# Second MLP: output product by seven block products, decoding inside PSUM, fixed ring slots

## The chip, the cores and the metric

One core of one Trainium2 chip. A core has five engines with instruction streams of their own: TensorE (PE: matmuls, with weight loads listed as PEld), VectorE (DVE), ScalarE (ACT), GpSimd (POOL) and SyncE (SP), which here issues the DMA transfers. Matmuls write to PSUM, a memory of eight banks; a bank holds 512 float32 columns on 128 partitions. VectorE and ScalarE read PSUM, GpSimd doesn't. The metric is the device time of one launch in microseconds, lower is better. This kernel was run three times: 957.83, 962.25 and 962.66 us.

## The reference

Three stages in float32, the output of one being the input of the next.

```python
# attention, 4 batches, 8 heads, 576 positions, 64 wide; causal by blocks of 64
attn = softmax(where(block_i >= block_j, q @ k.T / 8, -1e9));  x = attn @ v      # x: 2304 tokens x 512
# first MLP, 512 -> 2048 -> 512
h = x @ w_in;  x = (h * tanh(softplus(h))) @ w_out
# second MLP, 512 -> 1536 -> 512, with RMS norm
xn = x / sqrt(mean(x * x) + 1e-6) * rms_g
out = (silu(xn @ w_gate) * (xn @ w_val)) @ w_out
```

Inputs and weights come as 64-bit floats and are turned into 32-bit ones on the chip.

## The kernel before

**Precision.** A float32 operand is kept as two float16 halves, high and low. A product is three passes: high with high, high with low, low with high (`PASSES`).

**Second MLP, gate and value.** It runs by row blocks `n` (18 of them). Two row blocks, 256 rows of the hidden layer, are a block `l` = `n // 2` (9 of them); `l` goes over 3 weight blocks `fq` of 512 hidden rows and, inside each, 3 token blocks `p` of 768 tokens. In a row block, gate and then value are computed by a scheme of seven block products for eight (Strassen's, in Winograd's form): `quads("g")`, then `quads("v")`. The left operands are the weights (seven combinations, tiles of `row`, called `pair_row` outside), the right ones the normed tokens (seven combinations, 14 float16 column groups, loaded by transposing DMAs in `load_xn`). A `product` is 6 matmuls of 384 columns (L1790) into a PSUM bank of its own; the banks come in turn from two rings of two, `h` and `s`. The four results are put together outside PSUM: `copied` (ScalarE, L1808), `plus` (VectorE, L1818: a product read from PSUM plus a tile) and `both` (a sum of two tiles, VectorE or GpSimd, L1828). Gate results pass through Silu (L1840), value results are multiplied by them (L1846), and the product is split into a high half (L1853, L1854) and a low half (L1856): the tiles `pp`, in four rings of three or two.

**Second MLP, output.** `mlp2_o(l, pps)` multiplies the `pp` tiles of two row blocks by a block of `w_out`, as plain products: six output tiles of 128 tokens x 512 columns, for each 4 x 3 matmuls of 512 columns (L1925) into one of three banks. With `fq` = 0 ScalarE copies the bank into an accumulator in SBUF (L1935); after that VectorE adds to it (L1942). After the last `fq` the tile is stored (L1950).

**Weights.** `stage_w2` loads the three weights of one `fq`, rebuilds float32 from the 64-bit words by three integer operations on VectorE (L578, L586, L606), finds scales, and splits them; for `w_out` it makes two halves of the four plain pieces (`split`, L544 and L551). The next `fq` is staged while the present one is computed; for the last there is nothing to stage.

**Order of the work.** Nothing is issued in the order of the text. All operations are recorded first (`Plan.op`) with their engine or a choice of engines, an estimated duration and a due time (`at`). `Plan.place` simulates the engines with these estimates and takes, on each engine, the ready operation of the smallest key; `Plan.run` repeats that forward and backward for some rounds, adds tabled shifts (`SHIFT` by part of the program, `FINE` by operation), keeps the shortest plan and issues each engine's instructions in its order. At run time an engine follows that fixed order and waits at semaphores. An operation that reuses a tile of a ring waits for all uses of the tile that had the place before; in the second MLP the planner also holds the first use of a tile behind the first use of the tile before it in the ring (`b.after`). The products of gate and value, and the `plus` operations, are chained in their order (`chain`).

Of the kernel before, what the change touches and what calls it, by code (L numbers as in the profile page):

```python
# [47 lines left out]

class Buf:


    def __init__(self, pool, shape, dtype, name, tag, bufs):
        self.pool, self.shape, self.dtype, self.name, self.tag, self.bufs = pool, shape, dtype, name, tag, bufs
        self.ap, self.acc, self.prev, self.cols, self.whole, self.after = None, [], None, None, None, None
# [36 lines left out]
class Plan:  # L91


    def __init__(self):
        self.ops, self.rings, self.part, self.ordered = [], {}, "", False
# [16 lines left out]
    def op(self, eng, ns, fn, r=(), w=(), at=0.0, alts=(), after=(), table=None, issue=T_DGE):  # L112
# [15 lines left out]
        for acc, wr in ((r, False), (w, True)):  # L128
            for a in acc:
                b, part = split_part(a)  # L130
                if b.after is not None and not b.acc:
                    o.deps.update(p for p, _, _ in b.after.acc[:1])
                b.acc.append((o, part, wr))
# [4 lines left out]
    def place(self, key, back=False):  # L138
# [23 lines left out]
        while left:  # L162
# [160 lines left out]
def t_rows(n, nbytes):  # L323

    return n * {256: 12.0, 2048: 6.44, 4096: 13.44}[nbytes]
# [3 lines left out]
def block_attention_mish_mlp_gated_mlp(  # L329
# [37 lines left out]
    STEP2 = 21500.0  # L367
# [117 lines left out]
    def pow2_of_norm(cols, s, e, at, sl=ALL):  # L485
# [9 lines left out]
        pow2(c, None, (s, sl), (e, sl), 13, at)  # L495
# [295 lines left out]
    def split_k(b, a, pace):  # L791
# [6 lines left out]
        for tt in range(NTT):  # L798
# [9 lines left out]
                DMA, 1540.0 * n / P,  # L808
# [57 lines left out]
    def prep_q(b, tt, at):  # L866
# [15 lines left out]
        else:  # L882
# [13 lines left out]
            DMA, 1540.0 * n / P,  # L896
# [4 lines left out]
        op(DMA, 400, lambda: nc.sync.dma_start(out=w()[0:D, :, :n], in_=a()[D:P, :, :n]), r=[a], w=[(w, 0)], at=at)  # L901
        op(DMA, 400, lambda: nc.sync.dma_start(out=w()[D:P, :, :n], in_=a()[0:D, :, :n]), r=[a], w=[(w, 1)], at=at)
# [40 lines left out]
    def attention(b, i, at, pace):  # L943
# [113 lines left out]
        def probs(keys, es, at):  # L1057
# [50 lines left out]
            for z, e in enumerate(es):  # L1108
# [24 lines left out]
                DMA, 1.5 * wd,  # L1133
# [35 lines left out]
        def norm_x(half, xt, at):  # L1169
# [56 lines left out]
            if last:  # L1226
                for hh in range(2):
                    for s_ in range(2):
                        op(
                            DMA, 400,  # L1230
# [15 lines left out]
            for t, c0, jl, w in runs:  # L1246
                if t not in x16:
                    x16[t] = buf("m1", [P, 2 * NCC, T1], F16, f"x16_{t}", "x16", X_BUFS)
                op(
                    DMA, 770.0 * w,  # L1250
# [26 lines left out]
    op(DMA, 800, lambda: nc.sync.dma_start(out=rgb(), in_=rms_g.partition_broadcast(P)), w=[rgb], at=60000)  # L1277
# [183 lines left out]
    def norm(t, m, at):  # L1461
# [37 lines left out]
        def halves(pool, o0, o1, c0, part):  # L1499
# [4 lines left out]
            else:  # L1504
# [16 lines left out]
                DMA, {2: 824, 3: 1250}[w],  # L1521
# [58 lines left out]
    plan.ordered = True  # L1580
# [24 lines left out]
    def stage_w2(fq, at, pace, o_at, o_pace):  # L1605
# [4 lines left out]
        def stage(nm, src, z, at=at, pace=pace):  # L1610
# [18 lines left out]
            if nm == "o":  # L1629
                pow2_of_norm(sq, w2s[nm], w2E[nm], a, sl)  # L1630
# [16 lines left out]
            if nm == "o":  # L1647
                d = w2[nm, fq] = buf("m2", [P, FQ, 2, FW], F16, f"w2{nm}{fq}", f"wo{fq % 2}", 1)
                for cc in range(FQ):
                    split(  # L1650
                        lambda d=d, cc=cc: d()[:, cc, 0, :], lambda d=d, cc=cc: d()[:, cc, 1, :],
                        lambda big=big, cc=cc: big()[:, cc, :], s_, FW, d, [(big, cc), (w2s[nm], fq)], a, (cc, 1), (cc, 0),
                    )
# [10 lines left out]
        def row(nm, r, a):  # L1664
            plan.part = f"r{nm}{fq}_{r}"
            big = bigs[nm]
            y = (NR * fq + r) % 3
            d = w2[nm, fq, r] = buf("m2" if y == 2 else "w2", [P, 7, 2, 2, P], F16, f"w2{nm}{fq}_{r}", f"w{nm}{y}", 1)
# [3 lines left out]
            def put(o, r, src, rd):  # L1672
                hi, lo_ = lambda: d()[:, o, 0], lambda: d()[:, o, 1]
                n = 2 * P
                op(
                    ACT, t_act(n), lambda: nc.scalar.activation(out=hi(), in_=src(), func=AF.Copy), r=rd, w=[(d, (o, 0))],  # L1676
# [4 lines left out]
                    POOL, t_pool(n), lambda: lo(nc.gpsimd), r=rd + [(d, (o, 0))], w=[(d, (o, 1))], at=a,  # L1681
# [3 lines left out]
            def summed(o, r, i0, i1, rd, fn):  # L1685
                x = buf("w2", [P, 2, P], F32, f"w2s{nm}{fq}_{r}_{o}", "wsum6" if o == 3 else f"wsum{o}", 1)
# [10 lines left out]
            put(0, r, q[1, 1], rk_[1])  # L1697
            put(1, r, q[1, 2], rk_[2])
            put(2, r, q[2, 2], rk_[2])
            s1_ = summed(4, r, q[2, 1], q[2, 2], rk_[1] + rk_[2], ALU.add)  # L1700
            s2_ = summed(5, r, s1_, q[1, 1], [s1_] + rk_[1], ALU.subtract)
            summed(6, r, q[1, 1], q[2, 1], rk_[1], ALU.subtract)
            summed(3, r, q[1, 2], s2_, [s2_] + rk_[2], ALU.subtract)

        def scales_gv(a):
# [17 lines left out]
                    out=ck()[:, sl], in0=w2E["v"]()[:, sl], scalar1=gr(), scalar2=2.0**-16, op0=ALU.mult, op1=ALU.mult  # L1723
# [4 lines left out]
        def scale_o(a):  # L1728
# [7 lines left out]
            tiny(lambda: nc.vector.tensor_scalar_mul(co()[:, sl], g2(), 2.0**-15), [g2], [(co, fq)], a)  # L1736

        bigs = {}
        return (
            lambda: (stage("g", w_gate, 0), stage("v", w_val, FQ), scales_gv(at + pace * 2 * FQ)),  # L1740
            lambda r, a: (row("g", r, a), row("v", r, a)),
            lambda: (stage("o", w_out2, 0, o_at, o_pace), scale_o(o_at + o_pace * FQ)),
        )
# [3 lines left out]
    def load_xn(l, at):  # L1747
# [4 lines left out]
        for part, c0, c1 in ((0, 0, 2 * DM), (1, 2 * DM, 4 * DM), (2, 4 * DM, 7 * DM)):  # L1752
            for m in range(NM):
                r0 = (p * NM + m) * P
                op(
                    DMA, 1.5 * (c1 - c0),
# [8 lines left out]
    chain = {"PE": [], "DVE": [], "n": 0}  # L1765
    PRODUCTS = {1: (0, 0), 2: (1, 1), 3: (3, 2), 4: (2, 6), 5: (4, 3), 6: (5, 4), 7: (6, 5)}

    def mlp2_gv(n):
# [6 lines left out]
        def quads(nm):  # L1775
# [3 lines left out]
            bank = {}  # L1779

            def product(z):
                wo, xo = PRODUCTS[z]
                chain["n"] += 1
                b = bank[z] = (ps_h if chain["n"] % 2 else ps_s)([P, T2], f"{nm}{n}_{z}")

                def mm():
                    i = 0
                    for cc in range(2):
                        for wh, xh in PASSES:
                            nc.tensor.matmul(  # L1790
                                b(), w()[:, wo, wh, cc, :], x()[:, (2 * xo + xh) * 2 + cc, :],
                                start=(i == 0), stop=(i == 5),
# [4 lines left out]
                chain["PE"] = [op(PE, t_mm(T2, 6), mm, r=xs + [(w, (wo, 0)), (w, (wo, 1))], w=[b], at=a, after=chain["PE"])]  # L1797

            scale = (lambda: 1.0) if nm == "g" else (lambda: ck()[:, fq : fq + 1])
            sc_r = [] if nm == "g" else [(ck, fq)]  # L1800

            def copied(z, tag):

                d = buf("w2", [P, T2], F32, f"{tag}{nm}{n}", tag, 1)
                b = bank[z]
# [6 lines left out]
            def plus(z, u, name, d=None):  # L1812

                d = d or buf("w2", [P, T2], F32, f"{name}{nm}{n}", name, 1)
                b = bank[z]
                last = op(
# [4 lines left out]
                    r=[b] + ([] if d is u else [u]) + sc_r, w=[d], at=a, after=chain["DVE"],  # L1821
                )
                chain["DVE"] = [last]
                return d

            def both(u, v, name, d=None):
                d = d or buf("w2", [P, T2], F32, f"{name}{nm}{n}", name, 1)
                f = lambda eng: eng.tensor_tensor(out=d(), in0=u(), in1=v(), op=ALU.add)  # L1828
                op(
                    POOL, t_pool(T2), lambda: f(nc.gpsimd), r=[u] if d is v else [u, v], w=[d], at=a,  # L1830
                    alts=[(DVE, t_dvett(T2), lambda: f(nc.vector))],
                )
                return d

            def use(i, src):

                if nm == "g":
                    op(
                        ACT, t_act(T2, 1),
                        lambda: nc.scalar.activation(out=src(), in_=src(), func=AF.Silu, scale=cg()[:, fq : fq + 1]),  # L1840
# [358 lines left out]
```

## Time and profile before

| | |
|---|---|
| runs | 957.83, 962.25, 962.66 us; median 962.25 |
| the profiled execution | 958.27 us |
| its span, first to last instruction | 956.5 us |
| mean granted TensorE clock | 0.999 of full |
| instructions | 18899 |

The profile shows one execution. Busy time is the time in which an engine had at least one instruction in flight; matmuls are pipelined, so the mean duration of one is longer than the distance from one to the next. The first 550 us hold attention and the first MLP, interleaved; the second MLP begins at 557 us, and its last matmul ends 3.9 us before the span does.

### The profile page before, as it was taken

The numbers are of one execution on the slowest core, as the hardware profiler recorded it, in microseconds if no ns is written. First come the engines' busy times: TensorE is split into PE (matmuls) and PEld (weight loads), VectorE is DVE, ScalarE is ACT, GpSimd is POOL, SyncE is SP. The second block draws the span as 40 slices with busy tenths as digits, with TensorE's granted clock in tenths as the row PEclk, the third lists the DMA queues.
The fourth block names the chain that finished last, engine by engine and source line by source line (L and its number), as shares of the span: only waits on it lengthen the run. The fifth ranks groups of instructions, "written<-read, shape, count | busy, mean of one in ns | idle before, by whom it ended". The sixth has DMA issues, their size and how long they took to land. (4 is left out here: it accounts for less than half of the span.)

```text
span 956.5 us, 18899 instructions
## 1 busy us (share of the span) xinstructions
PE 932.2 (97%) x6754; PEld 585.3 (61%) x6755; DVE 785.3 (82%) x1797; ACT 600.5 (63%) x1244; POOL 509.9 (53%) x659
## 2 busy tenths in 40 slices
PE   8999999899999999999999999999999999999998
PEld 7785566466666758666675665555555555545553
DVE  5999978987896689988884999899989989765654
ACT  4769679998699889887775654647454635312320
POOL 1249245885562447577551936768555856412321
PEclk9999999999999999999999999999999999999999
DMA  9754698699875498788663747755658270552002
GB/s 228 217 199 129 187 159 151 125 153 174 141 143 101 86 178 167 134 180 154 149 144 57 144 127 138 172 133 94 156 126 141 75 148 15 103 110 73 12 34 88
DMA packets 317183, 125.37 MB, mean 131 GB/s; under 512 B 296353, under 2 KB 296353, under 8 KB 317089
## 3 DMA queue, kind: packets, MB, share of 16 engines
q1 hardware_dynamic: 317088, 124.17, 61.4%
q8 instruction: 53, 0.87, 0.4%
q14 instruction: 42, 0.34, 0.1%
HBM read 50.07 MB, written 12.98 MB: 66 GB/s over the span
## 5 line engine op out<-in xcount | busy, mean ns | idle before, releaser
L1378 PE MATMUL h<-x,w1i 128*128 128x256 f16 x1536 | 179.3, 273 | 1.3 <-ACT f L1404 1.3
L1439 PE MATMUL y<-w1o,g 128*128 128x512 f16 x768 | 178.5, 379 | 1.8 <-DVE w1o L551 1.7
L1378 PEld LDWEIGHTS <-w1i 128*128 128x128 f16 x1536 | 146.3, 98 | 23.1 <-issue 2.7
L1790 PE MATMUL g<-xnT,w2g 128*128 128x384 f16 x756 | 129.0, 326 | 0.0
L1790 PE MATMUL v<-xnT,w2v 128*128 128x384 f16 x756 | 126.9, 326 | 0.0
L1439 PEld LDWEIGHTS <-g 128*128 128x128 f16 x768 | 71.1, 98 | 80.5 <-issue 5.1
L1790 PEld LDWEIGHTS <-w2g 128*128 128x128 f16 x756 | 73.8, 98 | 51.5 <-issue 0.4
L1790 PEld LDWEIGHTS <-w2v 128*128 128x128 f16 x756 | 74.0, 98 | 50.3
L1018 DVE TENSOR_REDUCE mx<-s 128x1 f32<-128x512 f32 (+4 forms) x128 | 70.1, 557 | 19.7 <-PE s L984 17.8
L1043 ACT ACTIVATE e<-s,bias,cS 128x512 f32<-128x512 f32 (+4 forms) x120 | 72.5, 607 | 21.0 <-POOL bias L1027 11.0
L1421 DVE SCALAR_TENSOR_TENSOR g<-f,ich,g 128x512 f16<-128x512 f32 x64 | 55.4, 871 | 10.7 <-ACT g L1416 6.6
L1155 PEld LDWEIGHTS <-pt 128*128 128x128 f16 x1128 | 48.7, 98 | 22.2 <-DMA pt<-p 8.2
L1155 PE MATMUL x<-v,pt 128*128 128x64 f16 (+1 forms) x1128 | 55.5, 199 | 4.2 <-DMA pt<-p 3.4
L518 POOL TENSOR_SCALAR p<-e 128x128 f16<-128x128 f32 (+2 forms) x57 | 27.0, 474 | 57.7 <-ACT e L1043 39.6
L1124 POOL TENSOR_TENSOR p<-e,p 128x512 f16<-128x512 f32 (+4 forms) x54 | 50.4, 937 | 6.5 <-DVE p L1117 2.9
L1043 ACT ACT_TABLE_LOAD x38 | 48.8, 1283 | 4.6 <-DVE bias L1027 3.9
L1404 ACT ACTIVATE f<-h,ch 128x512 f32<-128x512 f32 x64 | 43.4, 684 | 10.4 <-PE h L1378 8.6
L1404 ACT ACT_TABLE_LOAD x38 | 48.8, 1283 | 1.1 <-issue 0.4
L1828 POOL TENSOR_TENSOR p5g<-u2g,p5g 128x384 f32<-128x384 f32 x15 | 15.9, 1058 | 58.3 <-DVE sl22g L1828 54.6
L1124 DVE TENSOR_TENSOR p<-e,p 128x384 f16<-128x384 f32 (+4 forms) x58 | 37.6, 650 | 8.4 <-ACT p L1120 4.9
L983 PE MATMUL s<-kT,qT 128*128 128x384 f16 (+3 forms) x96 | 27.5, 299 | 6.1 <-ACT e L1043 5.9
L1808 ACT ACTIVATE p5v<-v,ck 128x384 f32<-128x384 f32 x18 | 10.4, 580 | 36.5 <-PE v L1790 36.5
(612 smaller groups left out, 2155.5 us busy)
## 6 DMA issues: line engine op xcount, KB each, us to landing
wir<-in_moe_w_in_dram SPq DMA_DIRECT2D x16, 512.0 KB, 5.1
wor<-in_moe_w_out_dram SPq DMA_DIRECT2D x16, 512.0 KB, 3.9
w2rg<-in_moe_w_gate_dram SPq DMA_DIRECT2D x24, 256.0 KB, 3.4
w2rv<-in_moe_w_val_dram SPq DMA_DIRECT2D x24, 256.0 KB, 3.0
w2ro<-in_moe_w_out_dram SPq DMA_DIRECT2D x24, 256.0 KB, 3.4
q<-in_q_dram SPq DMA_DIRECT2D x16, 256.0 KB, 3.8
k<-in_k_dram SPq DMA_DIRECT2D x16, 256.0 KB, 4.1
v<-in_v_dram SPq DMA_DIRECT2D x15, 256.0 KB, 4.4
```

Source lines behind the costliest of these rows:

```text
L518: nc.gpsimd.tensor_scalar(out=out_, in0=in_, scalar1=by, scalar2=1.0, op0=ALU.mult, op1=ALU.mult)
L983: nc.tensor.matmul(t, src[b, i]()[:, h, :], kT[b]()[:, h, 0:n], start=(ph == 0), stop=False)
L1018: lambda z=z, cols=cols: nc.vector.reduce_max(out=mx()[:, cols], in_=ts[z](), axis=AX.X),
L1043: lambda y=y, z=z, c0=c0, w=w, acc=acc, e=e, h=h: nc.scalar.activation(out=e()[:, c0 : c0 + w], in_=ts[z]()[:, y, :], func=AF.Exp, bias=bi ...
L1124: lo = lambda eng, z=z, ev=ev: eng.tensor_tensor(out=view(p16)[:, z, :, 1, :], in0=ev(0, kt), in1=view(p16)[:, z, :, 0, :], op=ALU.subtract)
L1155: nc.tensor.matmul(xt()[:, cols, :], pv(z)[:, t, ph, :], v16[b, t]()[:, vh, key * w : key * w + w], start=(t == 0 and y == 0), stop=(t == ...
L1378: nc.tensor.matmul(ph()[:, g, :], w1i[fq]()[:, cc, wh, f * P : (f + 1) * P], x()[:, xh * NCC + cc, :], start=(z == 0), stop=(z == 3 * NCC ...
L1404: ACT, t_act(W, 1, True), lambda: nc.scalar.activation(out=e(), in_=phf(), func=AF.Mish, scale=cs()),
L1421: lambda: nc.vector.scalar_tensor_tensor(out=g16()[:, 1], in0=hv(), scalar=sc(), in1=g16()[:, 0], op0=ALU.mult, op1=ALU.subtract),
L1439: nc.tensor.matmul(yps[t, m](), g16()[:, gh, g, m * P : (m + 1) * P], w1o[f]()[:, wh, :], start=(f == 0 and z == 0), stop=(f == NF1 - 1 an ...
L1790: nc.tensor.matmul(b(), w()[:, wo, wh, cc, :], x()[:, (2 * xo + xh) * 2 + cc, :], start=(i == 0), stop=(i == 5),)
L1828: f = lambda eng: eng.tensor_tensor(out=d(), in0=u(), in1=v(), op=ALU.add)
```

## The change

1. **Output product.** For each token tile `m` of 128 (three per block) seven products replace eight: the left operands are seven combinations of the `pp` tiles (first and second half of tokens against first and second row block of each pair), the right ones seven combinations of the quarters of `w_out` (`out_quads`, in place of the four plain pieces). A product is 6 matmuls of 256 columns into one side of a bank; two banks, u and v, serve a token tile, and each is read between products that add to it.
2. **Operands.** After the value quad four sums are made in place of its four tiles, and seven tiles `pp` are split instead of four, in one ring of 14 places.
3. **Decoding of gate and value in PSUM.** Three banks a quad instead of seven: product 2 alone, products 1, 6, 7 and 4 on top of each other in bank u, with a read after each, 5 and then 3 in a third. `both` is gone; Silu and the multiplication of (2, 1) read PSUM directly. The tiles of the decoding move from the pool `w2` to `m2`, which opens when the first MLP's weights are released.
4. **Rings.** Every place of a ring has a tag of its own, so tile i always takes place i modulo the ring's length; `b.after` and `chain` go.
5. **Planner.** DMA estimates have two parts, time to land and time in the queue (`Moved`); `STEP2`, the due-time pace of a row block, goes from 21500 to 20600; 20 rounds for 10; new tables `SHIFT` and `FINE`.

Powers of two in the scales (13 to 11 and the like) change with the ranges of the operands.

```diff
     def buf(self, pool, shape, dtype, name, tag=None, bufs=1):
-        b = Buf(pool, shape, dtype, name, tag, bufs)
+        b = Buf(pool, shape, dtype, name, tag, 1)
...
-            if self.ordered and ring:
-                b.after = ring[-1]
+            b.tag = f"{tag}_{len(ring) % bufs}"
...
-                bus = end[i] = max(t + T_BUS, bus) + ns
+                bus = end[i] = max(t + T_BUS + ns - ns.queued, bus) + ns.queued
...
+            c2 = copied(b2, "c2")
+            u = bank("u")
+            product(1, u, True)
+            summed((1, 1), u, c2)
+            b5 = bank("5")
+            product(5, b5, True)
+            c5 = copied(b5, "c5")
+            product(6, u)
+            u2 = copied(u, "u2", 2)
+            product(7, u)
+            summed((2, 2), u, c5)
+            product(4, u)
+            use((2, 1), u)
+            product(3, b5)
+            summed((1, 2), b5, u2)
...
+                if i != (1, 2):
+                    halved({(1, 1): 0, (2, 1): 1, (2, 2): 2}[i], sl)
+                    return
+                a11, a12, a21, a22 = sls[1, 1], sls[2, 1], sls[1, 2], sls[2, 2]
+                for o, d, i0, i1, fn in (
+                    (6, a11, a11, a21, ALU.subtract), (4, a21, a21, a22, ALU.add),
+                    (5, a22, a22, a11, ALU.subtract), (3, a12, a12, a22, ALU.subtract),
+                ):
...
+                pp = pps[o] = buf("m2", [P, 2, T2], F16, f"pp{n}_{o}", "pp", PP_BUFS)
...
+            u, v = banks
+            product(1, u, 1, True)
+            product(2, u, 0)
+            begin(u, lambda u=u: u()[:, 1], h1(a1, 0), a1, HK)
+            product(4, v, 0, True)
+            product(5, v, 1)
+            begin(v, lambda v=v: v(), h2(a2), a2, DM)
+            product(6, u, 1)
             if fq == 0:
...
+                add(u, lambda u=u: u()[:, 0], h1(a1, 0), a1, HK)
+                first(u, lambda u=u: u()[:, 1], h1(a1, 1), a1, HK)
+            else:
+                add(u, lambda u=u: u(), h2(a1), a1, DM)
+            product(3, v, 1)
+            add(v, lambda v=v: v()[:, 1], h1(a1, 1), a1, HK)
+            product(7, u, 1)
+            add(u, lambda u=u: u()[:, 1].unsqueeze(1).to_broadcast([P, 2, HK]), h2(a2), a2, DM)
...
+WO_BUFS, PP_BUFS, W_BUFS, O_SPREAD = 8, 14, 18, 1.2
```

In `out_quads` four differences of quarters of `w_out` are made in place (VectorE or GpSimd, 512 columns each), and seven quarters are split into halves. `begin` is a ScalarE copy with `fq` = 0 and a VectorE add after that.

## Rows read from the trace of the kernel before

**Rows 1.** The page, part 1: busy us, share of the span, instructions.
```profile
PE 932.2 (97%) x6754; PEld 585.3 (61%) x6755; DVE 785.3 (82%) x1797; ACT 600.5 (63%) x1244; POOL 509.9 (53%) x659
```

**Rows 2.** Stretches: length, busy (x) of PE, PEld, DVE, ACT, POOL; clock, DMA.
```profile
550.00:600.00 50.00, 50.00 (x303) 29.32 (x301) 46.85 (x100) 24.53 (x46) 24.88 (x27) 1.00 0.60 134
600.00:800.00 200.00, 199.59 (x1117) 109.03 (x1116) 183.22 (x359) 105.44 (x215) 136.12 (x140) 1.00 0.57 123
800.00:956.50 156.50, 152.62 (x848) 82.54 (x846) 98.52 (x167) 43.72 (x86) 44.34 (x40) 1.00 0.28 66
```

**Rows 3.** Groups of matmuls and weight loads: count, busy us, mean ns, idle before.
```profile
L1378 PE MATMUL h<-x,w1i 128*128 128x256 f16 x1536 | 179.3, 273 | 1.3 <-ACT f L1404 1.3
L1378 PEld LDWEIGHTS <-w1i 128*128 128x128 f16 x1536 | 146.3, 98 | 23.1 <-issue 2.7
...
L1925 PE MATMUL o<-w2o,pp_(1, 2)_8966 128*128 128x512 f16 x9 | 2.4, 379 | 0.0
```

**Rows 4.** The chain that ended last, pieces: start us, us, what.
```profile
535.30 10.36 PE y L1439 x48
545.66 7.86 PE h L1378 x72
```

**Rows 5.** The same chain, the last value quad.
```profile
927.67 6.83 PE v L1790 x42
```

**Rows 6.** Timeline of one value quad's decoding: start us, us, instruction, idle before.
```profile
928.74 0.58 ACT L1808 ACTIVATE p1v<-v,ck 128x384 f32<-128x384 f32 x1 [4.59 <-PE v L1790]
929.73 0.62 DVE L1818 SCALAR_TENSOR_TENSOR u2v<-v,ck,p1v 128x384 f32<-128x384 f32 x1 [3.87 <-PE v L1790]
...
932.85 0.36 DVE L1853 CAST pp_(1, 1)_12850<-sl11g 128x384 f16<-128x384 f32 x1
933.25 0.56 DVE L1828 TENSOR_TENSOR u2v<-u2v,p5v 128x384 f32<-128x384 f32 x1
933.35 1.23 POOL L1856 TENSOR_TENSOR pp_(1, 1)_12850<-sl11g,pp_(1, 1)_12850 128x384 f16<-128x384 f32 x1 [10.44 <-DVE pp_(1, 1)_12850 L1853]
933.85 1.15 DVE L1828 TENSOR_TENSOR p5v<-u3v,p5v 128x384 f32<-128x384 f32 x1
```

**Rows 7.** Groups on VectorE, 600 to 800 us.
```profile
L1818 DVE SCALAR_TENSOR_TENSOR sl11g<-g,p1g 128x384 f32<-128x384 f32 x9 | 4.9, 544 | 0.0
L551 DVE SCALAR_TENSOR_TENSOR w2o<-w2fo,w2so,w2o 128x512 f16<-128x512 f32 x4 | 3.8, 1012 | 0.0
L1942 DVE SCALAR_TENSOR_TENSOR acc<-o,co,acc 128x512 f32<-128x512 f32 x4 | 3.0, 738 | 1.2 <-PE o L1925 1.2
```

**Rows 8.** A group on ScalarE, 600 to 800 us.
```profile
L1808 ACT ACTIVATE p1v<-v,ck 128x384 f32<-128x384 f32 x9 | 5.1, 569 | 4.6 <-PE v L1790 4.6
```

**Rows 9.** Timeline of VectorE: a read of 256 PSUM columns.
```profile
583.74 0.48 DVE L1493 SCALAR_TENSOR_TENSOR sums_b<-y,rk,rgb 128x256 f32<-128x256 f32 x1 [0.18 <-POOL rk L1488]
```

**Rows 10.** Busy time, 600 to 800 us, of L1828 alone: VectorE, then GpSimd.
```profile
600.00:800.00 200.00, 16.07 (x18) 19.30 (x18) 1.00 0.57 123
```

**Rows 11.** The same of L1942: VectorE.
```profile
600.00:800.00 200.00, 8.79 (x12) 1.00 0.57 123
```

**Rows 12.** The same of L1846, then of L1856: VectorE, then GpSimd.
```profile
600.00:800.00 200.00, 7.12 (x10) 28.34 (x26) 1.00 0.57 123
...
600.00:800.00 200.00, 15.38 (x16) 22.26 (x20) 1.00 0.57 123
```

**Rows 13.** Timeline of the end.
```profile
943.08 0.33 SPq L1950 DMA_DIRECT2D out_dram<-acc_xh  x1
...
952.66 0.75 DVE L1942 SCALAR_TENSOR_TENSOR sums_b<-o,co,sums_b 128x512 f32<-128x512 f32 x1 [1.84 <-PE o L1925]
```

**Rows 14.** A wait of TensorE: us in total, times, longest us.
```profile
PE x L1155 <- DMA pt<-p: 3.4, 7, 0.9
```

**Rows 15.** Timeline of TensorE where the second MLP begins.
```profile
565.38 6.99 PE L1790 MATMUL v<-xnT,w2v 128*128 128x384 f16 x42
572.20 6.64 PE L1439 MATMUL y<-w1o,g 128*128 128x512 f16 x30
```

More of the change, by code (lines that the diff above doesn't have):

```diff
@@ L1647, in stage @@
             if nm == "o":
[L1648 to L1653, printed above, removed]
+                bigs[nm] = big
                 return
@@ L1696, in row @@
             rk_ = {k: [(big, 2 * k - 2), (big, 2 * k - 1)] for k in (1, 2)}
[L1697 to L1703, printed above, removed]
+            if 0 in parts:
+                put(1, r, q[1, 2], rk_[2])
+                put(0, r, q[1, 1], rk_[1])
+                s1_ = summed(4, r, q[2, 1], q[2, 2], rk_[1] + rk_[2], ALU.add)
+                second[nm] = summed(5, r, s1_, q[1, 1], [s1_] + rk_[1], ALU.subtract)
@@ new lines, in row, with out_quads, put, less @@
+            if 1 in parts:
+                summed(6, r, q[1, 1], q[2, 1], rk_[1], ALU.subtract)
+                put(2, r, q[2, 2], rk_[2])
+                s2_ = second[nm]
+                summed(3, r, q[1, 2], s2_, [s2_] + rk_[2], ALU.subtract)
+        def out_quads(a):
+            plan.part = f"2wq{fq}"
+            nm, big = "o", bigs["o"]
+            s_ = lambda: w2s[nm]()[:, sl]
+            half = lambda k, c: (lambda: big()[:, k - 1 : FQ : 2, (c - 1) * HK : c * HK])
+            b11, b12, b21, b22 = half(1, 1), half(1, 2), half(2, 1), half(2, 2)
+            rk = {k: [(big, k - 1), (big, k + 1)] for k in (1, 2)}
+            w2[nm, fq] = ds = [None] * 7
+            def put(o, src, k):
+                d = ds[o] = buf("m2", [P, 2, FQ // 2, HK], F16, f"w2{nm}{fq}_{o}", "wo", WO_BUFS)
+                split(
+                    lambda: d()[:, 0], lambda: d()[:, 1], src, s_, FW, d, rk[k] + [(w2s[nm], fq)], a, 1, 0,
+                )
+            def less(dst, i0, i1, k):
+                f = lambda eng: eng.tensor_tensor(out=dst(), in0=i0(), in1=i1(), op=ALU.subtract)
+                op(
+                    DVE, t_dvett(FW), lambda: f(nc.vector), r=rk[3 - k], w=rk[k], at=a,
+                    alts=[(POOL, t_pool(FW), lambda: f(nc.gpsimd))],
+                )
+            put(0, b11, 1)
+            put(1, b21, 2)
+            put(2, b22, 2)
+            less(b11, b12, b11, 1)
+            put(3, b11, 1)
+            less(b12, b22, b12, 1)
+            put(5, b12, 1)
+            less(b22, b22, b11, 2)
+            put(4, b22, 2)
+            less(b21, b21, b22, 2)
+            put(6, b21, 2)
@@ L1778, in quads, with bank, product @@
             w = w2[nm, fq, r]
-            bank = {}
-            def product(z):
+            g = nm == "g"
+            def bank(name):
+                chain["n"] += 1
+                return (ps_h if chain["n"] % 2 else ps_s)([P, T2], f"{nm}{n}_{name}")
+            def product(z, b, first=False):
                 wo, xo = PRODUCTS[z]
-                chain["n"] += 1
-                b = bank[z] = (ps_h if chain["n"] % 2 else ps_s)([P, T2], f"{nm}{n}_{z}")
                 def mm():
@@ L1796, in product, with tile_of, copied @@
                 xs = [(x, (m, (0, 0, 1, 1, 2, 2, 2)[xo])) for m in range(NM)]
[L1797 to L1805, printed above, removed]
+                op(PE, t_mm(T2, 6), mm, r=xs + [w[wo]], w=[b], at=a)
+            scale = (lambda: 1.0) if g else (lambda: ck()[:, fq : fq + 1])
+            sc_r = [] if g else [(ck, fq)]
+            def tile_of(name, bufs=1):
+                return buf("m2", [P, T2], F32, f"{name}{nm}{n}", name, bufs)
+            def copied(b, name, bufs=1):
+                d = tile_of(name, bufs)
                 op(
@@ L1820, in plus @@
                     ),
-                    r=[b] + ([] if d is u else [u]) + sc_r, w=[d], at=a, after=chain["DVE"],
+                    r=[b] + ([] if d is u else [u]) + sc_r, w=[d], at=a,
                 )
[L1823 to L1833, printed above, removed]
```

281 lines of the change are left out of this document (153 added, 128 removed), and 312 rows, old and new, of tables (FINE, SHIFT).

## The prediction

> **What bounds the kernel now.** First the page's busy shares: TensorE is busy for 932.2 of 956.5 us, VectorE 82%, ScalarE 63%, GpSimd 53% [rows 1]. Busy matmul time flatters, so I asked for stretches next. From 550 to 800 us TensorE idles 0.4 us, and the 3.9 us missing after 800 us lie behind the last matmul [rows 2]; that leaves 932.2 - 402.2 = 530.0 busy and 20 us idle in the 550 us of attention and first MLP. So the second MLP, the part that is changed, is bound by the stream of matmuls alone. The reader must also see VectorE there: 46.9 of 50 us in 550 to 600, 183.2 of 200 in 600 to 800, but 98.5 of 156.5 after that, when no weights are staged any more. It is the second engine, close behind the first. Third, the groups of matmuls give the counts [rows 3]; a group's mean (326 or 379 ns) is latency, not spacing. Spacing comes from long unbroken pieces in the chain of waits [rows 4, 5]: 48 matmuls of 512 columns in 10.36 us are 215.8 ns each, 72 of 256 columns in 7.86 us are 109.2 ns, 42 of 384 columns in 6.83 us are 162.6 ns. The clock is full in all of them [rows 2].
>
> **Output product.** Before: 9 blocks l, six output tiles each, 4 x 3 matmuls of 512 columns, 648 in all: 648 x 215.8 ns = 139.8 us. After: 9 blocks, three token tiles m, seven products of 6 matmuls, 256 columns: 1134 x 109.2 ns = 123.8 us. That is -16.0 us, all of it on the bound engine. The weight load does not spoil it: 256-column matmuls already stand in the first MLP with a 98 ns load each [rows 3], and their spacing of 109.2 ns was taken with these loads under them.
>
> **Gate and value.** The same 1512 matmuls of 384 columns: 0 us of TensorE work. What changes is who reads PSUM, and when. Before, each of seven products had a bank, four banks took turns, and a product waited only for a reader several products back. Now products 1, 6, 7 and 4 go into one bank u with a reader between each pair. The trace of before shows no matmul waiting for a reader in the middle of a chain, so I bound it. A reader starts about 0.1 us after its product: product 1 of the value quad at 927.67 [rows 5] ends 0.98 us later, at 928.65, and its copy starts at 928.74 [rows 6]. A VectorE read lasts 0.62 us, and I count 0.1 us back to TensorE: 0.82 us from one product to the next in u. Product 5 (0.98 us) stands in the first gap, product 3 in the second, and only product 2 of the next quad is there for the third. Free below: 0 us, if VectorE always answers at once. Above: rival D. The value I take: VectorE's instructions in 600 to 800 us last 183.2/359 = 0.51 us on average and it is 92% busy, so a read that is due finds it in the middle of another one; spread evenly over 0 to 0.51 us, less the 0.15 us that the covering product leaves over, that is 0.12 us a read, and as some last 1.15 us [rows 6] I take 0.17. For even row blocks, products of the output (0.65 us each) cover this. For odd ones little of them is left, because the ring of 14 operand tiles holds two row blocks, so the output products of block l must be through before the value quad of the next block can store. Two VectorE reads a quad, two quads, six blocks with weights still being staged: 24 x 0.17 = 4.1 us, taken as 4.
>
> Here the trace and a rule can be weighed. The trace has no row of a product that continues a bank just read. The Trainium skill, "PSUM — Partial Sum Buffer", section "Summary: rules for kernel authors", speaks against it: while a matmul runs, read a different bank, and guard with semaphores by bank. By that rule each step of u is a full hand-over and nothing overlaps, which is rival D, below; no run here shows it yet.
>
> **Work of the other engines.** Per row block VectorE loses 3 of 10 decode adds (0.55 us for gate [rows 7], 0.62 for value [rows 6]) and its share of 4 plain adds; ScalarE gains two copies (0.57 us [rows 8]) and loses none. Added are 4 sums of operands, 3 more low halves (1.23 us on GpSimd [rows 6]) and 3 more high halves (0.36 us on VectorE [rows 6], or ScalarE). The accumulation costs most: before 3 adds of 512 a row block (0.74 us [rows 7]); after, with fq above 0, per token tile three reads of 512 and two of 256 (0.48 us, the price of the 256-column read in [rows 9]): 3 x 0.74 + 2 x 0.48 = 3.2 us; with fq = 0, 1.7 us on VectorE. For 600 to 800 us (nine row blocks of decode, five blocks of output) VectorE loses 18 x 0.55 + 9 x 0.62 = 15.5 and the 16.1 us of plain adds [rows 10], and gains 9 x 1.7 + 6 x 3.2 - 8.8 = 25.7 us of accumulation [rows 11], 7 us for sums at the split between engines that the multiplications had [rows 12], 11.5 us for 12 of the 27 new low halves at today's 0.96 [rows 12], and 7 us for three more halves of w_out (1.01 us each [rows 7]) and four differences per weight block: about +20, 203 us, while the stretch shrinks to 191.7. With the new sums and low halves all on GpSimd it is 184, and GpSimd has 136.1 - 19.3 [rows 10] - 9 vanished multiplications and + 63 new operations, all at 1.1 us [rows 12]: 176. So it fits, at 96% and 92%. This is the ground for the 4 us, and for rival C. ScalarE has room (105.4 of 200).
>
> **The tail.** After the last matmul, one VectorE add of 0.75 us and one store remain [rows 13]. New: the last read feeds both output tiles, so a second store is issued behind the first, 0.33 us [rows 13]. In the last token tile product 7 waits for the read of product 6, with only product 3 (0.65 us) to cover 0.1 + 0.75 + 0.1 and a read of v ahead of it: 0.5 us. The last value quad has nothing behind it: 0.8 us in its third gap. Its late operand sums come one by one, while only five early output products (3.3 us) stand in front: 0.5 us. Sum +2.2; bounds 0.4 (all covered but the store) and 4.
>
> **The rest.** Loads, attention and first MLP compute the same; their order is written anew by the planner, from other transfer prices, other due times, and rings whose slots have fixed places. TensorE waits there 3.4 us for transposes [rows 14]. A better guess of transfers could take the 3.4 away, a worse one double it: I take 0, bounds -3.5 and +3.5. The decode tiles moved to the pool that opens when the first MLP's weights are released. Before, the first value quad, for one, ran ahead of the first MLP's last 30 matmuls [rows 15]; after, these go first, and only products 2, 1 and 5 can run before the pool opens. The work is the same and TensorE has enough of it: 0; if an operand of the last step comes late, +2.
>
> **Sum.** -16.0 + 4.0 + 2.2 = -9.8 us. The profiled execution took 958.27 us, so 948.5 on its footing. The median of the runs is 962.25, 4 us above the profiled run; I predict against the median: 952.4 us.
>
> **Rivals.** B, the gain arrives whole: the planner places output products into all gaps and the tail costs 1 us: -15, 947. For: TensorE idles 0.2% in 600 to 800 us today with VectorE at 92%. Against: the gaps are new, and shorter than a VectorE instruction can be late.
>
> C, VectorE becomes the bound while weights are staged: with the split of today it needs 203 us where 191.7 are there, 11 us per 200, over the 255 us from 575 to 830 some 14 us. -16 + 14 + 2.2 = 0, so 962.5, no change. For: GpSimd, which must take the overflow, slows VectorE: a plain add took 0.56 us alone and 1.15 us beside GpSimd's 1.23 [rows 6]. Against: there is room on GpSimd and ScalarE, and the sums are offered to either engine.
> The Trainium skill, "SBUF — State Buffer", section "Who interferes with whom", names the same: a VectorE instruction with two SBUF inputs contends with a GpSimd instruction that reads SBUF. By that rule sums moved off VectorE stretch those that stay, and the time leans to C; the trace agrees, with 1.15 against 0.56 us.
>
> D, slower: the lock step between value and gate. The next gate quad writes its first sum into a tile that the sums of the value quad before it still read. From the value quad's last product to the gate's product 6: read 0.62, multiply 0.56, sum 0.56, high half 0.36, low half 1.23 on GpSimd, first sum 0.55, and seven hand-overs of 0.1: 4.6 us. TensorE's own work in it is three products, 2.9 us; 1.7 us are bare. At nine of the 18 boundaries the next output block covers it; at the other nine the old one is already spent. 9 x 1.7 = 15: -16 + 15 + 4 + 2.2 = +5.2, 967.5. It decides from 1.1 us per boundary upward. For: the ring of 14. Against: the last products of the old block may still run there, 1.3 us of cover.
>
> That the change does not do what it says (no fewer columns streamed) is excluded by the counts, 1134 x 256 against 648 x 512.
>
> **How the numbers follow.** About 0.5% (4.8 us) is what a measurement here can tell from no change. A, the forecast, with its own range 948 to 957: 0.42. B 0.25. C 0.18. D 0.15. Faster (below 957.4): A without its upper edge 0.37, B 0.25, some of C 0.04: 0.66. Same: 0.05 of A, 0.12 of C, 0.03 of D: 0.20. Slower: 0.14. Low end: B with the 3.5 us of attention and 2.5 us for the lower of the runs shown, 941. High end: below D's middle, 965.
>
> **What would show it.** Right: 1134 output matmuls of 256 columns in runs spaced 109 ns; TensorE idle of some 5 us between 600 us and the end that the waits put down to VectorE; VectorE above 90% while weights are staged, GpSimd far above its 68% of 600 to 800 us. Waits of matmuls on ScalarE copies alone would mean that the second gap, not the first and third, is the thin one. B is shown by no such idle time, C by VectorE at 97% and TensorE in steps behind it, D by bare pieces of 1 to 2 us at every second boundary from value to gate. The prediction is wrong if the stretch before 550 us moves by more than 4 us, or if the spacing at 256 columns is above 112 ns.

## The result, and the profile after

The changed kernel took 952.52 us (median of 6 runs, 951.63 to 953.17); the kernel before took 960.82 us beside it (6 runs, 957.83 to 962.75). The ratio is 0.9916, with a 95% interval of 0.9893 to 0.9939: faster by 0.8%. The forecast was 952.4 us. The profiled pair differs less: 951.73 against 958.27 us, spans 949.9 against 956.5, so 6.6 us are there to be accounted for in the traces.

Page, part 1, of the changed kernel (against [rows 1]), and its stretches (against [rows 2], same columns, with the stretch before 550 us):

```profile
PE 921.5 (97%) x7241; PEld 632.4 (67%) x7241; DVE 807.5 (85%) x1837; ACT 657.5 (69%) x1369; POOL 550.8 (58%) x688
```

```profile
0.00:550.00 550.00, 528.54 (x4504) 365.54 (x4505) 459.76 (x1187) 437.01 (x919) 311.70 (x453) 1.00 0.75 154
550.00:600.00 50.00, 49.78 (x282) 27.27 (x280) 41.50 (x82) 28.30 (x51) 30.39 (x30) 1.00 0.60 134
600.00:800.00 200.00, 198.70 (x1413) 137.78 (x1411) 190.18 (x379) 126.72 (x271) 148.47 (x150) 1.00 0.54 115
800.00:949.90 149.90, 144.50 (x1048) 101.83 (x1045) 116.02 (x194) 65.51 (x129) 60.20 (x58) 1.00 0.31 73
```

In 600 to 800 us TensorE works 198.7 us and VectorE 190.2, 95% where it was 92%. Next, the group of output matmuls, and two unbroken pieces of it in the chain of waits (start, us, what; against [rows 3, 4]):

```profile
L1989 PE MATMUL o<-w2o,pp 128*128 128x256 f16 x1134 | 138.6, 273 | 2.2 <-DVE pp L1899 1.2
```

```profile
863.58 6.58 PE o L1989 x60
...
906.01 3.93 PE o L1989 x36
```

36 matmuls in 3.93 us are 109.2 ns each, 60 in 6.58 us 109.7. The shares of the chain by engine (page, part 4) show what is new; in the kernel before TensorE held 45% of this line and VectorE 1%:

```profile
PE 31%; DVE 10%; POOL 3%; ACT 3%; issue 1%; DMA 1%; DVEq 0%; POOLq 0%; ACTq 0%
```

Most of the lost time is not in the idle column. In the timeline of TensorE at the start of the second MLP, six matmuls of gate or value should start 0.98 us apart:

```profile
580.21 1.14 PE L1830 MATMUL g<-xnT,w2g 128*128 128x384 f16 x6
581.19 1.14 PE L1830 MATMUL v_u<-xnT,w2v 128*128 128x384 f16 x6
...
585.20 1.14 PE L1830 MATMUL g_u<-xnT,w2g 128*128 128x384 f16 x6
586.39 1.14 PE L1830 MATMUL g<-xnT,w2g 128*128 128x384 f16 x6
587.61 3.08 PE L1830 MATMUL g_u<-xnT,w2g 128*128 128x384 f16 x18
```

The first two do; the next three start 1.19 and 1.22 us apart. But a row lasts 1.14 us, 0.17 more than its six spacings, so that only 0.05 and 0.08 us of these gaps of 0.21 and 0.24 count as idle. I therefore count from 560 us on: matmuls left (by line, in the window from 560 us) times their spacing, against the time to the end of the last matmul, 3.8 us before the span's end. Before: 36 x 0.2158 + 1497 x 0.1626 + 648 x 0.2158 = 391.0 us of work in 392.7. After, with 35 matmuls of the first MLP, 1512 of gate and value and 1134 of 256 columns, 377.2 us in 386.1. TensorE is **without work** for 8.9 us instead of 1.7 (some 1 us of either figure are 11 small matmuls that the count leaves out). Of these, 2.3 lie in the tail (126 output matmuls, 13.8 us of work, take 16.0), 1.1 between 575 and 600 us, the rest in many gaps of 0.4 us at most. This is the tail (timeline of TensorE):

```profile
929.93 4.04 PE L1989 MATMUL o<-w2o,pp 128*128 128x256 f16 x35
934.72 0.83 PE L1989 MATMUL o<-w2o,pp 128*128 128x256 f16 x6 [0.74 <-DVE pp L1899]
935.99 5.52 PE L1989 MATMUL o<-w2o,pp 128*128 128x256 f16 x49 [0.44 <-DVE pp L1899]
941.70 3.44 PE L1989 MATMUL o<-w2o,pp 128*128 128x256 f16 x30 [0.19 <-DVE sums_b L2010]
945.32 0.81 PE L1989 MATMUL o<-w2o,pp 128*128 128x256 f16 x6 [0.19 <-DVE sums_b L2010]
```

At 560 us the changed kernel is 2.2 us behind: 7.6 us of the first MLP are left to do, before 7.8 less 2.4 of the second done ahead. Sum: -16.0 + 7.2 + 2.2 = -6.6 us, the difference of the spans.

### The profile page after: what moved, and what is told of

Read it like the earlier page. It is cut to its first block, busy times and chain, and to the rows that moved or that the text cites. A ratio compares the mean times of both kernels' runs of the same rounds, so it can differ in the third digit from the quotient of the medians.

```text
span 949.9 us, 20061 instructions
## 1 busy us (share of the span) xinstructions
PE 921.5 (97%) x7241; PEld 632.4 (67%) x7241; DVE 807.5 (85%) x1837; ACT 657.5 (69%) x1369; POOL 550.8 (58%) x688
## 5 line engine op out<-in xcount | busy, mean ns | idle before, releaser
L1989 PE MATMUL o<-w2o,pp 128*128 128x256 f16 x1134 | 138.6, 273 | 2.2 <-DVE pp L1899 1.2
L1989 PEld LDWEIGHTS <-pp 128*128 128x128 f16 x1134 | 110.5, 98 | 26.3 <-issue 3.2
L1830 PE MATMUL v_u<-xnT,w2v 128*128 128x384 f16 x432 | 81.5, 326 | 0.3 <-DVE wc L659 0.2
L1830 PE MATMUL g_u<-xnT,w2g 128*128 128x384 f16 x432 | 78.9, 326 | 0.3
L1130 POOL TENSOR_TENSOR p<-e,p 128x384 f16<-128x384 f32 (+4 forms) x61 | 58.5, 960 | 18.2 <-DVE p L1123 6.8
L1427 DVE SCALAR_TENSOR_TENSOR g<-f,ich,g 128x512 f16<-128x512 f32 x64 | 57.9, 910 | 8.9 <-ACT g L1422 6.3
L1830 PE MATMUL v<-xnT,w2v 128*128 128x384 f16 x324 | 61.5, 326 | 0.0
L1830 PE MATMUL g<-xnT,w2g 128*128 128x384 f16 x324 | 61.1, 326 | 0.2
L1130 DVE TENSOR_TENSOR p<-e,p 128x512 f16<-128x512 f32 (+4 forms) x51 | 39.3, 773 | 4.1 <-ACT p L1126 2.5
```

Of the source, the lines that this page charges most:

```text
L1130: lo = lambda eng, z=z, ev=ev: eng.tensor_tensor(out=view(p16)[:, z, :, 1, :], in0=ev(0, kt), in1=view(p16)[:, z, :, 0, :], op=ALU.subtract)
L1427: lambda: nc.vector.scalar_tensor_tensor(out=g16()[:, 1], in0=hv(), scalar=sc(), in1=g16()[:, 0], op0=ALU.mult, op1=ALU.subtract),
L1830: nc.tensor.matmul(b(), w[wo]()[:, wh, cc, :], x()[:, (2 * xo + xh) * 2 + cc, :], start=(first and i == 0), stop=(i == 5), skip_group_chec ...
L1989: nc.tensor.matmul(b()[:, side, :], pps[r][po]()[:, gh, m * P : (m + 1) * P], w[wo]()[:, wh, r, :], start=(first and i == 0), stop=(i == 5 ...
```

## The experiments

Theory: the output product gives its 16 us, and VectorE, hardly faster than TensorE while weights are staged, gives part of it back by late reads. Rivals: the hand-overs in one bank cost by themselves; TensorE alone is the bound and VectorE has room.

**e1: fewer columns in the kernel before.** 11 of 12 output matmuls stream 442 columns instead of 512, nothing else.

```diff
+                        cols = DM if g == 0 and i == 0 else 442
...
-                            y(), pp()[:, gh, m * P : (m + 1) * P], w2["o", fq]()[:, g, wh, :],
+                            y()[:, :cols], pp()[:, gh, m * P : (m + 1) * P], w2["o", fq]()[:, g, wh, :cols],
```

> The kernel before, with its own plan, but the output matmuls stream fewer columns: the first of each tile 512, the other eleven 442, 448 on average (an eighth of the output's columns is left out). Nothing else changes. Theory: TensorE alone bounds the second MLP, so 648 x 64 columns at 2.4 per ns, 17.3 us, come off whole: about 943.5 against 960.8. Rival: the other engines are close enough behind that less work on TensorE is worth only half of itself here: about 952, with new waits of TensorE on VectorE.

946.64 us (945.2 to 949.5), ratio 0.9857 (0.9811 to 0.9902): -13.9 of the 17.3 us, nearer to the theory's -17 than to the rival. From 560 us TensorE has 375.8 us of work and takes 383.9: 8.1 us without work, nearly as many as the changed kernel, although decode and order are the old ones. That is one execution, at 949.5 us the slowest of the four; by the medians 3.4 of the 17.3 us are lost. In 600 to 800 us:

```profile
600.00:800.00 200.00, 196.00 (x1137) 110.70 (x1136) 184.43 (x364) 106.10 (x219) 138.58 (x142) 1.00 0.59 125
```

So it is not the new hand-overs that TensorE needs in order to wait: a TensorE that is 17 us faster runs up against the others. TensorE's order in e1 is that of the kernel before, instruction for instruction; still e1 is 2.1 us behind it at 560 us. Two profiles of one order differ by that much there.

**e2 and e3: VectorE lighter and heavier.** Two of the three integer operations that rebuild weights, for the later weight blocks: in e2 on 8 of 256 columns; in e3 one of them is issued twice. TensorE's order is unchanged in both.

```diff
-                out=dst().bitcast(U32), in0=word(0), scalar=29, in1=dst().bitcast(U32),
+                out=dst().bitcast(U32)[:, :cut], in0=word(0)[:, :cut], scalar=29, in1=dst().bitcast(U32)[:, :cut],
...
-            lambda: nc.vector.scalar_tensor_tensor(
+            lambda: [nc.vector.scalar_tensor_tensor(
...
+            ) for _ in range(2 if cut else 1)],
```

> The changed kernel, same plan and order, but while the weights of the second and third weight block are staged two of the three integer operations per piece (96 in all) work on 8 of 256 columns, so those weights are not right. VectorE gets some 40 us lighter between 575 and 830 us. Theory (the bare gaps of TensorE between products there, some 4 us, are VectorE coming late): they go, 948.5 against 952.5. Rival (the gaps are the hand-over itself: product, read, next product in one bank): under 1 us, 952.

> The changed kernel, same plan and order, but the third integer operation per piece is issued twice for the second and third weight block (48 more operations of about 0.5 us, 24 us of VectorE between 575 and 830 us; the result is the same). Theory: VectorE is 96% busy there and TensorE is bare whenever it is late, so 8 to 14 us come on top: 960 to 966. Rival (hand-over, VectorE has room): under 2 us, 954.

e2: 950.22 us (949.84 to 951.18), ratio 0.9892 (0.9841 to 0.9942). e3: 977.78 us (976.87 to 978.62), ratio 1.0177 (1.0133 to 1.022). The stretch of 600 to 800 us in e2, then in e3:

```profile
600.00:800.00 200.00, 198.86 (x1421) 138.64 (x1420) 175.47 (x380) 127.38 (x272) 144.90 (x151) 1.00 0.55 114
```

```profile
600.00:800.00 200.00, 183.61 (x1274) 123.96 (x1272) 190.74 (x379) 116.93 (x247) 130.77 (x131) 1.00 0.52 109
```

With 15 us less on VectorE in this stretch TensorE is without work for 7.4 us instead of 8.9; with 48 operations more, for 33.1. By the medians the two sides are very unequal: 2.3 us gained, 25.3 lost. e2 lies between its theory (948.5) and its rival (952), e3 well above its theory (960 to 966). The changed kernel stands just on the edge at which VectorE becomes the bound. But e2 does not make VectorE lighter everywhere. In 750 to 800 us it is still busy for 47.6 of 50 us, and TensorE's gaps there stay (0.8 us in the changed kernel, 0.9 in e2):

```profile
750.00:800.00 50.00, 49.77 (x346) 33.62 (x344) 47.63 (x88) 30.62 (x70) 42.87 (x48) 1.00 0.37 72
```

**e4: the late operand sums.** For the last row block the four sums run on 8 of 384 columns; the other columns of these operands are left as they were.

```diff
+                    w_ = 8 if n == NR * NL - 1 else T2
-                    f = lambda eng, d=d, i0=i0, i1=i1, fn=fn: eng.tensor_tensor(out=d(), in0=i0(), in1=i1(), op=fn)
+                    f = lambda eng, d=d, i0=i0, i1=i1, fn=fn, w_=w_: eng.tensor_tensor(out=d()[:, :w_], in0=i0()[:, :w_], in1=i1()[:, :w_], op=fn)
```

> The changed kernel, same plan, but the four operand sums of the last row block work on 8 of 384 columns (its last operands are not right). Theory: the two largest bare stretches of the end (0.74 and 0.44 us of waiting for a low half) are the chain of these sums; they shrink by 1 us, 951.5. Rival: the end is set by the reads of the accumulating banks: no change, 952.5, and the wait moves to them.

950.73 us (949.45 to 951.27), ratio 0.9894 (0.9851 to 0.9936); its tail:

```profile
928.82 4.66 PE L1990 MATMUL o<-w2o,pp 128*128 128x256 f16 x41
933.84 5.52 PE L1990 MATMUL o<-w2o,pp 128*128 128x256 f16 x49 [0.36 <-DVE pp L1900]
939.55 3.43 PE L1990 MATMUL o<-w2o,pp 128*128 128x256 f16 x30 [0.19 <-DVE sums_b L2011]
943.17 0.81 PE L1990 MATMUL o<-w2o,pp 128*128 128x256 f16 x6 [0.19 <-DVE sums_b L2011]
```

The 126 matmuls now take 15.0 us: 1.2 without work instead of 2.3. The sums cost 1.1 us of the tail. The other 1.1 us by which this span is shorter (947.7 against 949.9) lie ahead of 560 us, where nothing differs.

**e5 to e8: each part alone, on equal footing.** The tables `SHIFT` and `FINE` are emptied in all four; e5 has the old decode and the old output product, e6 the new decode only, e7 the new output product only, e8 both. Against the changed kernel, e8 is only this:

```diff
-SHIFT = {
...
+SHIFT = {}
-FINE = {
...
+FINE = {}
```

e6 has `mlp2_o` and the four plain pieces of `w_out` of the kernel before besides; e7 has `alone`, `plus` and `both` of the kernel before in place of the products in bank u; e5 has all of these. In e5 and e6 the ring of operands has 12 places, three row blocks of four; in e7 and e8 it has 14, two row blocks of seven. The planner makes an order of its own for each of the four.

> Four kernels on equal footing (e5 to e8): the two hand-kept tables that shift the planner's due times are emptied in all four, with the same rings, transfer prices and number of rounds of the planner, and each of the two parts of the change is in or out. This one has neither: old decode in SBUF, old output product of eight blocks. Its own time is only a zero: some 955 to 975. What counts are the differences. Theory, the two parts depend on each other: output product alone +16, decode alone 0 to +4, both -9. Rival, each part counts by itself: output product alone -14 (its TensorE work less the 2 us of the tail), decode alone +5, both -9.

> The decode of gate and value by accumulation in PSUM, with the old output product. VectorE loses adds that it does not need to lose, since the output product of eight blocks leaves it at 92%. Theory: 0 to +1 us against e5, the hand-overs being hidden where VectorE has time to answer. Rival, each hand-over costs by itself: +4 to +5 us against e5.

> The output product of seven blocks, with the old decode in SBUF. By the prices of the trace of before VectorE would need, from 600 to 800 us, 183.2 + 25.7 for accumulation + 7 for halves of w_out and differences, with all new sums and low halves on GpSimd: 216 where 191.7 are there, 24 per 200 us, some 30 us over the 255 us in which weights are staged. Theory: -16 + 30 + 2 = +16 us against e5 (+10 to +30), with VectorE above 94% and TensorE idle in that stretch. Rival, TensorE stays the bound: -14 us against e5.

> Both parts, without the tables. Theory and rival: -9 us against e5 (the same change as between the two kernels of the study, with no order tuned by hand), 0 to 550 us equal within 2 us in e5 and e8. If instead the tables made the gain: 0 against e5.

| | median us (runs) | against e5 | TensorE's work from 560 us | without work |
|---|---|---|---|---|
| e5, neither | 966.76 (965.13 to 967.4) | | 399.8 | 1.1 |
| e6, decode | 967.47 (966.36 to 968.32) | +0.7 | 399.2 | 2.0 |
| e7, output | 1006.29 (1003.94 to 1008.65) | +39.5 | 389.0 | 54.1 |
| e8, both | 970.40 (969.41 to 971.39) | +3.6 | 387.4 | 17.6 |

Stretches of 600 to 800 us of e6, e7 and e8:

```profile
600.00:800.00 200.00, 200.00 (x1126) 109.82 (x1124) 152.72 (x326) 110.21 (x222) 85.10 (x93) 1.00 0.53 116
```

```profile
600.00:800.00 200.00, 182.58 (x1220) 121.43 (x1218) 185.65 (x338) 107.08 (x216) 164.89 (x157) 0.96 0.44 95
```

```profile
600.00:800.00 200.00, 195.45 (x1384) 134.87 (x1382) 193.50 (x370) 128.64 (x270) 151.92 (x151) 1.00 0.58 115
```

The parts depend on each other, as the theory had it. The new decode alone takes VectorE from 179.5 us (e5) to 152.7 and costs nothing measurable (+0.7): hand-overs in bank u are free where VectorE has time to answer. The new output product with the old decode loses 39.5 us, more than twice what I expected, with VectorE at 93%, not above 94%. Not all of it is waiting: the granted clock is 0.96 in this stretch, which is some 8 us of full speed. The decode in PSUM is what makes room for the output product. But both together do not gain either: without the tables TensorE saves 16.0 us of work, loses 16.5 more than e5 without work, and comes to 560 us 3.6 us later. Equality ahead of 550 us was expected; nearly half of the 3.6 is the clock, 0.67 in 535 to 540 us where e5 has 1.00. Theory and rival both expected -9 there and both fell; what I had listed as a third way, that the tables make the gain, came out: they are worth 17.9 us to the changed kernel (970.40 against 952.52).

**e9 to e11: what the order has to do with it.** In e9 products 6, 7, 4 and 3 go each to a bank of its own, and the accumulation is left out. e10 is e9 with the light VectorE of e2, e11 is e8 with it.

```diff
-            product(6, u)
+            u = bank("6")
+            product(6, u, True)
...
-            product(7, u)
+            u = bank("7")
+            product(7, u, True)
...
-            product(4, u)
+            u = bank("4")
+            product(4, u, True)
...
-            product(3, b5)
+            b5 = bank("3")
+            product(3, b5, True)
```

> The changed kernel, in which products 6, 7, 4 and 3 of each gate and value quad go each to a bank of its own out of the ring of four and begin a sum of their own there. The accumulation is left out (gate and value are not the reference's); every matmul, read and sum is still issued with the same sizes. From 560 us to its last matmul the changed kernel's TensorE is without work for 8.9 us, 2.3 of them in the tail. Theory, the hand-overs product, read, product in one bank make the idle time: 948.5 (-4), some 2 us of idle time left before 925 us. Rival, VectorE's sheer load makes it, whatever the banks: 952.5, no change.

> Both at once: products 6, 7, 4 and 3 in banks of their own (the accumulation is left out), and the two VectorE operations that put a w2 tile's words together on 8 of 256 columns for the later weight blocks (as in e2; those weights are wrong in the other columns). Theory, the two causes are the same one, a VectorE read that comes late: 947 (-5.5), the idle time of 560 us to the tail under 2 us. Rival, the idle time belongs to the order of the work and to operand waits: 950, as with the light VectorE alone.

> The changed kernel without the two tables (e8), with the two VectorE operations of e2 on 8 of 256 columns for the later weight blocks. e8 loses 17.4 us of TensorE time behind 560 us where e5 loses 1.1. Theory, VectorE's load, in an order that is not fitted to it, makes these 17: they fall to 9 or less, 961 to 962 (-9 against e8's 970.4). Rival, the order itself leaves TensorE without operands: 969 to 970.

e9: 959.84 us (958.64 to 964.2), ratio 1.0013 (1.0002 to 1.0025). e10: 951.52 (951.05 to 952.14), ratio 0.9923 (0.9911 to 0.9935). e11: 964.35 (963.43 to 964.83), ratio 1.0055 (1.0041 to 1.0069). Without work from 560 us: 13.1, 6.0 and 11.9 us.

Theory and rival of e9 fell: taking the hand-overs away did not gain 4 us but lost 7.3. It is no clean test, since the planner rewrote the whole order and e9 is 3.7 us behind the changed kernel at 560 us. Up to 3.4 us of that are the clock: 0.66 in 135 to 140 us, 0.87 and 0.79 in 525 to 535 us. But it shows how a loss can come about. Timeline of VectorE and TensorE in e9:

```profile
681.10 0.81 DVE L584 TENSOR_SCALAR w2fo<-w2ro 128x256 uint32<-128x256 uint32 x1
681.83 0.41 DVE L612 SCALAR_TENSOR_TENSOR w2fo<-w2ro,w2fo 128x256 uint32<-128x256 uint32 x1
682.16 0.41 DVE L592 SCALAR_TENSOR_TENSOR w2fo<-w2ro,w2fo 128x256 uint32<-128x256 uint32 x1
682.50 0.76 DVE L584 TENSOR_SCALAR w2fo<-w2ro 128x256 uint32<-128x256 uint32 x1
683.17 0.89 DVE L612 SCALAR_TENSOR_TENSOR w2fo<-w2ro,w2fo 128x256 uint32<-128x256 uint32 x1
683.98 0.41 DVE L592 SCALAR_TENSOR_TENSOR w2fo<-w2ro,w2fo 128x256 uint32<-128x256 uint32 x1
684.32 0.28 DVE L584 TENSOR_SCALAR w2fo<-w2ro 128x256 uint32<-128x256 uint32 x1
684.52 0.60 DVE L1911 SCALAR_TENSOR_TENSOR c2v<-v_u,ck,c2v 128x384 f32<-128x384 f32 x1
...
685.18 3.48 PE L1830 MATMUL v<-xnT,w2v 128*128 128x384 f16 x12 [2.99 <-DVE c2v L1911]
```

The read of bank v_u, whose product ended at 681.2, stands in VectorE's fixed order behind seven operations that rebuild the next weights (the first had just begun), and TensorE stands idle for 2.99 us until the read. TensorE waits for none of those seven. In this same order e10 shortens such operations and gains 8.3 us, more than half of it at this one wait and in the lower clock behind it; as it, too, is 3.5 us behind at 560 us, it stays above both 947 and 950. e11 gains 6.1 on e8, between the theory's 9 and the rival's 0 to 1. In the changed kernel's own order the same saving gives 2.3 (e2). So how much of VectorE's load reaches TensorE depends on the order. That it is the place of the reads in VectorE's order is shown for the one wait above and fits the rest. It is not all: these are the two largest groups of TensorE's waits in e8 from 560 us on (us in total, times, longest), the first of them for a copy on ScalarE, of which e11 leaves 3.0 us. No run varies ScalarE's order.

```profile
PE g L1830 <- ACT c5g L1849: 3.5, 5, 1.2
PE g L1830 <- DVE sl21g L1867: 1.5, 1, 1.5
```

**e12: a version meant to be better.** In the last block, token tiles 1 and 2 take banks from the ring of gate and value.

```diff
-            for _ in range(2):
+            for y in range(2):
+                if l == NL - 1 and m + y > 1:
+                    chain["n"] += 1
+                    banks.append((ps_h if chain["n"] % 2 else ps_s)([P, 2, HK], f"o{l}_{m}_{y}"))
+                    continue
```

> A version meant to be better, nothing left out: in the last output block, token tiles 1 and 2 take their banks from the ring of gate and value, which has nothing left to do by then, and so need not wait for the reads of tile 0. The two last waits of 0.19 us for VectorE adds go, the 0.5 us hand-over of product 7 stays. 951.5 (-1) if the banks made those waits; 952.5 if the late operand sums make all of the tail, since products then wait for these instead.

951.56 us (950.35 to 952.14), ratio 0.9919 (0.9905 to 0.9932), against 0.9916 for the changed kernel: no difference that can be told. Its tail:

```profile
932.36 4.81 PE L1993 MATMUL o<-w2o,pp 128*128 128x256 f16 x41
937.41 7.22 PE L1993 MATMUL o<-w2o,pp 128*128 128x256 f16 x61 [0.24 <-POOL pp L1899]
945.12 0.81 PE L1993 MATMUL o<-w2o,pp 128*128 128x256 f16 x6 [0.50 <-DVE sums_b L2014]
```

The two waits of 0.19 us are one of 0.50 now, and the tail is without work for some 1.6 us instead of 2.3. If that is a gain, it is 0.7 us.

## Why the prediction was right

**Output product, -16.0.** Right: 1134 matmuls at 109.2 to 109.7 ns.

**Gate and value, +4.** Right in size. Without work from 560 us are 8.9 us; less the tail (2.3), the 1.7 of before and the 1.1 at the start, 3.8 remain. That VectorE's late reads can make such gaps is shown (e3, e9 with e10, e8 with e11). That they make all 3.8 is not: e2 took away 15 us of VectorE's work and 1.5 of the 8.9. Nor are the gaps where the 4 us were counted. Between 575 and 930 us, 31 matmuls start more than 0.05 us later than the spacing lets them, 5.7 us together. By the semaphores in the trace 1.4 us of this end with VectorE's reads of products 1 and 7 in bank u, the only ones in the sum; 1.4 with VectorE's reads of the output's banks, for which there was no term outside the tail; 1.1 with other VectorE instructions and 1.9 with ScalarE. So the size is luck in part, and what a less loaded VectorE would leave of it stays open. That the gaps would be "put down to VectorE" by the waits was too simple: most are shorter than what a matmul's row hides, and e6 shows that the hand-over as such has no price.

**Work of the other engines.** "It fits, at 96% and 92%": VectorE came to 190.2 of 200 us, 95%; its accumulation took 32.3 us against my 34.5. GpSimd came to 148.5, 74%, not 92%. The mis-sized term is the split: I gave GpSimd all new sums and low halves, and VectorE made 33 of the 68 low halves of that stretch. One reading was wrong as well: the add taken as 0.56 us "alone" lies beside GpSimd's 1.23 us for 0.46 of them [rows 6]. It began first, and the add of 1.15 us began second; the rows don't give a general price of GpSimd for VectorE. What I did not see is that "it fits" was no property of the sums: e8 has the same work, VectorE at 97%, and fits so badly that the gain is gone. I took the order as given to follow the work; it was a part of the change with a price of its own.

**The tail, +2.2.** 2.3 without work before the last matmul; behind it 3.77 us are left as against 3.88, so the second store costs nothing, and the last value quad shows no gap either. In their place the operand sums cost 1.1, not 0.5 (e4), and 1.2 remain with the hand-overs of products at the end.

**The rest, 0, and the start, 0 or +2.** 1.1 us between 575 and 600 us, and 2.2 behind at 560 us. The latter can't be told from nothing, since e1 has the order of before and lies 2.1 behind as well. These two are what the profiled pair is short of: -9.8 was forecast, -6.6 is the difference of the spans.

**Sum and median.** The medians differ by 8.3, the profiled pair by 6.5; on the footing of that pair 948.5 was forecast, and 951.73 came. That the time came within 0.2 us is luck in part: the median from which I counted, 962.25, was 1.4 above that of six runs.

**Rivals.** B, the whole gain, is refuted by the 8.9 us. C, VectorE as the bound, which I gave 0.18, is what e3 runs into. e8 has its signs, VectorE at 97% and 17.6 us without work that undo the gain, but a lighter VectorE (e11) still leaves 11.9 of them, so load is only a part there. The changed kernel escapes narrowly, by its order. D, a lock step of 1 to 2 us at every second boundary, is not there: no wait of TensorE in the second MLP is above 0.74 us, and ahead of the tail no gap is above 0.41.

## What to carry to other kernels

When work is taken from an engine that bounds a kernel and given to one that is 92% busy, work out the second engine's load, but don't stop at its sum: ask what stands in its order ahead of the reads that the first engine waits for, because with VectorE at 95 to 97% the order alone decided whether the same work took 952.5 or 970.4 us. Test such an edge from both sides, with the second engine a little lighter and a little heavier. And count matmuls times spacing against the clock: idle time as the profile shows it missed most of the loss here.

## What was unexpected of the hardware

Behind the wait of 2.99 us in e9 the granted clock fell. Stretches of 5 us of e9:

```profile
680.00:685.00 5.00, 2.11 (x12) 1.17 (x12) 5.00 (x11) 2.42 (x6) 3.08 (x5) 1.00 0.36 107
685.00:690.00 5.00, 4.82 (x21) 2.55 (x21) 5.00 (x11) 3.83 (x9) 3.25 (x4) 0.66 0.53 158
690.00:695.00 5.00, 5.00 (x42) 3.92 (x41) 4.56 (x14) 3.01 (x7) 3.62 (x4) 1.00 1.05 175
```

A mean of 0.66 between the levels 2.4 and 1.2 GHz is 3.4 us of the five at the lower one: 21 matmuls where the next 5 us hold 42. The wait cost about 1.7 us more than its length. A wait of 1.5 us in e8's second MLP left the clock at 1.00, and so did one of 2.3 us in e3 (timeline, then the stretch behind it):

```profile
717.59 0.81 PE L1989 MATMUL o<-w2o,pp 128*128 128x256 f16 x6 [2.30 <-ACT sums_b L2003]
```

```profile
720.00:725.00 5.00, 5.00 (x39) 3.58 (x37) 5.00 (x8) 3.60 (x8) 4.35 (x5) 1.00 0.01 3
```
